# Converting the float64 weights in place: raw words in the slots of their halves, three word operations in a PSUM bank, and the first k and v issued by ACT

## The chip, the cores and the metric

The kernel runs on one core of one Trainium2 chip. The metric is the device time of the program in microseconds (us), the median over runs of the same program. A profile is one execution of it, recorded by the hardware profiler. Engines are called as in the profile: PE is TensorE (PEld its weight loads), DVE is VectorE, ACT is ScalarE, POOL is GpSimd, SP is SyncE, which here only issues DMAs.

## The reference: block-causal attention, then a feed-forward layer with a rational activation

```
scores = (q @ k^T) / 8                     # 8 batches x 8 heads, 576 tokens, head size 64
scores = where(block_i >= block_j, scores, -1e9)      # blocks of 64 tokens
attn   = exp(scores - max);  attn = attn / (sum(attn) + 1e-9)
x      = (attn @ v) -> 4608 tokens x 512
h      = x @ w_in                          # 512 x 2048, w_in and w_out are float64
g      = (a0 + a1 h + a2 h^2 + a3 h^3) / (1 + |b0||h| + |b1|h^2 + 1e-6)
out    = g @ w_out                         # 2048 x 512
```

q, k and v are float32. The weights arrive as float64, and the kernel reads them as pairs of 32-bit words: w0 is the low word and w1 the high one.

## The kernel before

**Attention.** The 64 heads are taken as 32 pairs of two. A pair has five row tiles (in the order 4, 3, 2, 0, 1) and two heads, which makes ten steps (`items`, L636), and `attn_steps` (L638) runs through them. For each step PE computes a score tile into a PSUM bank of the pool `ps_a` (five banks), DVE takes the row maximum out of it (L511, or L507 for the last half of tile 4), ACT takes the exponential with its sum (L522), POOL adds the guard to the sum (L530), DVE inverts it (L531), and POOL scales the row (L534). PE then transposes the probabilities (L560) into a bank that `bank` (L464) hands out, and for the first six pairs ACT copies the bank to SBUF (L571) and PE multiplies it in full float32 with v (L583, L587). For later pairs the probabilities are split into a high and a low half. `load` (L363) fetches q and k of a pair, `prep` (L401) transposes and splits them, and `vprep` (L441) fetches or splits v; all DMAs go out on SP's queue. For the first four pairs `bank` cycles through four sources: `ps_a`, the two banks of `ps_o` and the one bank of `ps_h`. Up to twelve pairs also issue three dummy matmuls before a transpose (L557).

**Feed-forward.** It has two phases over the hidden dimension: phase A takes the first 1280 of 2048 columns (NFA = 10 blocks of 128) in chunks of 256 tokens, and runs among the attention steps; phase B takes the remaining 768 (NFB = 6 blocks) in chunks of 512 tokens after the attention. One unit of phase A computes h (`first`, L192, matmuls on L204, into the one bank of `ps_h`, tag "a"), which ACT and DVE read (L211, L213, L219, L220), then the activation, then `second` (L255, matmuls on L272). x and g and the weights are each split into a high and a low fp32r half, and three of the four products are taken. Phase A starts at step 52, when the first batch (four pairs) has its x in DRAM (`xscr`).

**The weights.** A "place" is one quarter of two 128-blocks: 128 partitions by 512 float64 values, 512 KB. Phase A has 20 places and phase B 12. `split_weights` (L114) handles a place as follows. SP loads the raw words into a staging tile (tag "os", two buffers, shared with the output tiles; L121). ACT takes the absolute value of the high words as floats (L126) into the tile `at` (tag "u", two buffers). DVE then works on `at` in SBUF: a maximum with the smallest allowed exponent (L127), a shift with a mask (L129), the upper three bits of the low word shifted in (L131), and the sign put back (L133). ACT writes the rounded high half (L138) and POOL subtracts to get the low half (L139). For phase B the two halves go to DRAM (L143 to L146) and come back after the attention (L722). The main loop (L699) asks for a place at chosen steps: phase A's at steps 9, 18, 27, 36 and then 44 to 59, phase B's from step 80 on.

**What sets the order.** The engines' instruction orders are fixed when the program is built: the framework simulates the program and puts on each engine, at every moment, the first instruction in program order whose inputs and buffers are ready. So an instruction can stand well ahead of its place in the program if its buffers are free, and a conversion stands ahead of its step wherever the staging tiles let it. At run time every engine, and SP's queue too, works strictly in that order.

Of the kernel before, what the change touches and what calls it, by code (L numbers as in the profile page):

```python
# [2 lines left out]

# [6 lines left out]
F32 = mybir.dt.float32  # L10
F32R = mybir.dt.float32r
I32 = mybir.dt.int32
U32 = mybir.dt.uint32
AF = mybir.ActivationFunctionType
ALU = mybir.AluOpType
# [4 lines left out]
B, H, S, D = 8, 8, 576, 64  # L20
# [6 lines left out]
LEND = 4  # L27
RL = 3
C0 = 0
EV = 6  # L30
DP = 12
DN = (3, 0, 0, 0, 0)
# [16 lines left out]
NFA = 10  # L49
# [9 lines left out]
MASKS = ((None, None), (0, 0), (0, 1), (1, 0))  # L59
QC = 1.0 + 1e-6  # L60

WMIN = struct.unpack("<f", struct.pack("<I", (1023 - 127) << 20))[0]


@with_exitstack
def attn_ffn_kernel(
# [39 lines left out]
    b0, b1 = bab[:, 0:1], bab[:, 1:2]  # L106


    def weight_tiles(pool, f0, nf, dt):
        wi = [pool.tile([128, 4, nf * 128], dt, name=f"wi{x}{f0}", tag=f"wi{x}") for x in "hl"]  # L110
        wo = [pool.tile([128, nf, DM], dt, name=f"wo{x}{f0}", tag=f"wo{x}") for x in "hl"]
        return wi + wo

    def split_weights(pool, f0, nf, dt):  # L114
        wih, wil, woh, wol = weight_tiles(pool, f0, nf, dt)

        def place(dhi, dlo, src, nm):

            nd, n = src.shape[1:]
            st = ffn.tile([128, 512, 2], I32, name=f"st{nm}", tag="os")  # L120
            nc.sync.dma_start(out=st.rearrange("p (d f) t -> p d (f t)", d=nd), in_=src.bitcast(I32))  # L121
            w0, w1 = st[:, :, 0], st[:, :, 1]
            at = ffn.tile([128, 512], F32, name=f"wa{nm}", tag="u")
            ai = at.bitcast(I32)

            nc.scalar.activation(out=at, in_=w1.bitcast(F32), func=AF.Abs)  # L126
            nc.vector.tensor_scalar_max(at, at, WMIN)  # L127

            nc.vector.tensor_scalar(out=ai, in0=ai, scalar1=3, scalar2=0x3FFFFFF8,  # L129
                                    op0=ALU.logical_shift_left, op1=ALU.bitwise_and)  # L130
            nc.vector.scalar_tensor_tensor(out=ai, in0=w0, scalar=29, in1=ai,  # L131
                                           op0=ALU.logical_shift_right, op1=ALU.bitwise_or)
            nc.vector.scalar_tensor_tensor(out=ai, in0=w1, scalar=-0x40000000, in1=ai,  # L133
                                           op0=ALU.bitwise_and, op1=ALU.bitwise_or)

            v3 = lambda x: x.rearrange("p (d f) -> p d f", d=nd)
            if dt is F32R:
                nc.scalar.copy(out=dhi, in_=v3(at))  # L138
                nc.gpsimd.tensor_tensor(out=dlo, in0=v3(at), in1=dhi.bitcast(F32), op=ALU.subtract)  # L139
            else:  # L140
                bt = ffn.tile([128, 512], F32R, name=f"wb{nm}", tag="v")
                pt = ffn.tile([128, 512], F32R, name=f"wp{nm}", tag="s")
                nc.scalar.copy(out=bt, in_=at)  # L143
                nc.gpsimd.tensor_tensor(out=pt, in0=at, in1=bt.bitcast(F32), op=ALU.subtract)
                nc.sync.dma_start(out=dhi, in_=v3(bt).bitcast(F32))
                nc.sync.dma_start(out=dlo, in_=v3(pt).bitcast(F32))  # L146

        def steps():
            for f in range(0, nf, 2):
                cs = slice(f * 128, f * 128 + 256)  # L150
                for d in range(0, 4, 2):
                    src = w_in[d * 128:(d + 2) * 128, (f0 + f) * 128:(f0 + f + 2) * 128]
                    place(wih[:, d:d + 2, cs], wil[:, d:d + 2, cs],
                          src.rearrange("(d p) f -> p d f", p=128), f"i{f0}_{f}_{d}")
                    yield
                for d in range(f, f + 2):
                    place(woh[:, d:d + 1, :], wol[:, d:d + 1, :],
                          w_out[(f0 + d) * 128:(f0 + d + 1) * 128, :].rearrange("(d p) e -> p d e", p=128),
                          f"o{f0}_{d}")
                    yield  # L160

        return (wih, wil, woh, wol), steps()


    class Ffn:
# [24 lines left out]
                self.x[ph, c] += [x[:, d] for d in range(nd)]  # L190

        def first(self, ph, c, u):  # L192
            wih, wil, _, _ = self.w[ph]
            xs = self.x[ph, c]
            tag = f"{ph}_{c}_{u}"
            pool = self.pools[self.n % len(self.pools)]
# [1 line left out]
            h = hp.tile([128, NBU[ph], CTS[ph]], F32, name=f"h{tag}", tag="a", bufs=1 if hp is ps_h else 3)  # L198
            for j in range(NBU[ph]):
                f = NBU[ph] * u + j  # L200
                fs = slice(f * 128, (f + 1) * 128)
                for dc in range(4):
                    for i, (w, hl) in enumerate(((wih, 1), (wih, 0), (wil, 0))):
                        nc.tensor.matmul(h[:, j, :], lhsT=w[:, dc, fs], rhs=xs[dc][:, hl, :],  # L204
                                         start=(dc == 0 and i == 0), stop=(dc == 3 and i == 2))
            self.n += 1
            hf = h.rearrange("p j t -> p (j t)")
# [45 lines left out]
                nc.gpsimd.tensor_tensor(out=gl, in0=st, in1=gh.bitcast(F32), op=ALU.subtract)  # L253

        def second(self, ph, c, u):  # L255
            _, _, woh, wol = self.w[ph]
            gh, gl = self.g.pop((ph, c, u))
            nu = NU[ph]
            nm = CTS[ph] // 128
# [7 lines left out]
            for j in range(NBU[ph]):  # L267
                f = NBU[ph] * u + j
                for m in range(nm):
                    ms = slice(m * 128, (m + 1) * 128)  # L270
                    for i, (g, w) in enumerate(((gh, woh), (gh, wol), (gl, woh))):
                        nc.tensor.matmul(self.o[m], lhsT=g[:, j, ms], rhs=w[:, f, :],  # L272
                                         start=(u == 0 and j == 0 and i == 0),
                                         stop=(u == nu - 1 and j == NBU[ph] - 1 and i == 2))
            if u == nu - 1:
# [53 lines left out]
    with ExitStack() as actx:  # L329
# [33 lines left out]
        def load(p):  # L363
            b, hp = divmod(p, NPAIR)
            h0 = 2 * hp
            qr, kr = ((ffn.tile([128, 4, 2, D], F32, name=f"{n}r{p}", tag="x", bufs=XB) if p < RL else
                       att.tile([128, 4, 2, D], F32, name=f"{n}r{p}", tag="raw", bufs=2)) for n in "qk")
            tr = att.tile([128, 2, D], F32, name=f"tr{p}", tag="tr", bufs=1)
            if p >= EV:
                vr = att.tile([128, 2, 5, D], F32, name=f"vr{p}", tag="vr", bufs=1)  # L370
            for i, (raw, src) in enumerate(((qr, q), (kr, k))):
                for j in range(2):
                    nc.sync.dma_start(out=raw[:, :, j, :],
                                      in_=src[b, h0 + j, 0:512, :].rearrange("(c p) d -> p c d", p=128))
                nc.sync.dma_start(out=tr[64 * i:64 * i + 64], in_=src[b, h0:h0 + 2, 512:S, :].rearrange("j p d -> p j d"))
            if p < EV:
                st_[p] = dict(qr=qr, kr=kr, tr=tr)
                return
            for j in range(2):
                nc.sync.dma_start(out=vr[:, j, 0:4, :],  # L380
                                  in_=v[b, h0 + j, 0:512, :].rearrange("(c p) d -> p c d", p=128))
            nc.sync.dma_start(out=vr[0:64, :, 4, :], in_=v[b, h0:h0 + 2, 512:S, :].rearrange("j p d -> p j d"))
            st_[p] = dict(qr=qr, kr=kr, tr=tr, vr=vr)
# [57 lines left out]
        def vprep(p):  # L441
            if p < EV:
                b, hp = divmod(p, NPAIR)
                for j in range(2):
                    js, src = slice(64 * j, 64 * j + 64), v[b, 2 * hp + j]
                    nc.sync.dma_start(out=vz[:, 0:4, j, js], in_=src[0:512].rearrange("(c p) d -> p c d", p=128))
                    nc.sync.dma_start(out=vz[0:64, 4, j, js], in_=src[512:S])
                return
            if p == EV:
                late()  # L450
# [13 lines left out]
        def bank(p, name):  # L464

            if p < LEND:
                nbank[0] += 1
                pool, tag = ((ps_a, "a"), (ps_o, "o0"), (ps_o, "o1"), (ps_h, "a"))[nbank[0] % 4]
            else:
                pool, tag = ps_a, "a"  # L470
            return pool.tile([128, 512], F32, name=name, tag=tag)
# [196 lines left out]
                yield k  # L668
            assert not todo

        wts, wsteps = split_weights(wpool, 0, NFA, F32R)
        load(0)
        for _ in range(C0):
            next(wsteps)
# [1 line left out]
        prep(0, 1)  # L676
        vprep(0)
        ff = Ffn()
        ff.w[0] = wts
        fsteps = ff.steps()  # L680
        done = 0

# [5 lines left out]
                done += 1  # L688

        KB = NPAIR * 10  # L690
        wscr, wstepsB = split_weights(dpool, NFA, NFB, F32)
        NWA, NWB = 2 * NFA, 2 * NFB
        wdone = C0
        WSTEPS = [0] * C0 + [(W0 * (i + 1)) // 4 for i in range(4 - C0)] + [WA + WD * i // 4 for i in range(NWA - 4)]
# [16 lines left out]

    wB = ctx.enter_context(tc.tile_pool(name="wB", bufs=1))
    ffb = ctx.enter_context(tc.tile_pool(name="ffb", bufs=2))
    wtsB = weight_tiles(wB, NFA, NFB, F32R)
    ff.w[1] = wtsB
    ff.ready = NCH
    ps_b = ctx.enter_context(tc.tile_pool(name="ps_b", bufs=1, space=PSUM))
    ff.pools, ff.hpools = [ffn, ffb], [ps_h, ps_b]
    for f in range(0, NFB, 2):
        for i, (d, s) in enumerate(zip(wtsB, wscr)):  # L720
            at = (slice(None), slice(None), slice(f * 128, f * 128 + 256)) if i < 2 else (slice(None), slice(f, f + 2))
            nc.sync.dma_start(out=d[at].bitcast(F32), in_=s[at])  # L722
    for _ in fsteps:
        pass

# [29 lines left out]
```

## Time and profile before

| what | value |
|---|---|
| median of 3 runs (lowest, highest) | 1302.56 us (1300.33, 1307.7) |
| the profiled execution, its span | 1301.48 us, 1299.6 us |
| PE busy | 1252.8 us (96% of the span) |
| DVE, ACT, POOL busy | 71%, 71%, 69% |
| mean granted TensorE clock | 0.994 of full |
| conversion of a phase A place begins on ACT | at 14.4 us the first, at 131.6 us the last |
| conversion of phase B's places ends | at about 606 us |

The span runs from the first to the last instruction. "Busy" is the time in which an engine executes; matmul ends are modelled. An idle stretch of an engine is put down to the releaser that came last. In the view of windows each row gives, for a stretch of time, the busy time of every engine with its number of instructions, the granted clock, the busy share of the DMA engines and their rate.

### The profile page before, as it was taken

The numbers are of one execution on the slowest core, as the hardware profiler recorded it, in microseconds if no ns is written. First come the engines' busy times: TensorE is split into PE (matmuls) and PEld (weight loads), VectorE is DVE, ScalarE is ACT, GpSimd is POOL, SyncE is SP. The second block draws the span as 40 slices with busy tenths as digits, with TensorE's granted clock in tenths as the row PEclk, the third lists the DMA queues.
The fourth block names the chain that finished last, engine by engine and source line by source line (L and its number), as shares of the span: only waits on it lengthen the run. The fifth ranks groups of instructions, "written<-read, shape, count | busy, mean of one in ns | idle before, by whom it ended". The sixth has DMA issues, their size and how long they took to land.

```text
span 1299.6 us, 22697 instructions
## 1 busy us (share of the span) xinstructions
PE 1252.8 (96%) x7644; PEld 1058.3 (81%) x7644; DVE 923.2 (71%) x1735; ACT 927.8 (71%) x2047; POOL 895.6 (69%) x1041
## 2 busy tenths in 40 slices
PE   6879899999999999999999999999999999999997
PEld 4657788888878888888888888897998888888886
DVE  5896667776887768778667677754656776666765
ACT  5776778877788777878868777876776655555553
POOL 4665668777777778787767676766677666666564
PEclk8999899999999999999999999999999999999999
DMA  6675243544443453543434333247111333443423
GB/s 156 179 203 146 67 138 87 142 114 139 123 114 96 137 151 93 151 114 100 116 82 111 90 84 96 72 145 264 61 49 49 107 105 130 130 130 130 147 81 106
DMA packets 210355, 153.80 MB, mean 118 GB/s; under 512 B 137792, under 2 KB 176704, under 8 KB 210240
## 3 DMA queue, kind: packets, MB, share of 16 engines
q1 hardware_dynamic: 210176, 152.36, 40.3%
q8 instruction: 61, 1.00, 0.3%
q14 instruction: 54, 0.44, 0.1%
q0 software_dynamic: 64, 0.00, 0.0%
HBM read 98.57 MB, written 44.04 MB: 110 GB/s over the span
## 4 chain that ended last, share of the span: by engine, by line
PE 74%; DVE 8%; ACT 7%; POOL 5%; DMA 3%; issue 2%; SPq 2%; POOLq 0%; ACTq 0%; DVEq 0%
PE h L204 28%; PE o L272 27%; PE o L626 5%; PE t L560 4%; PE s L500 3%; PE s L497 2%; ACT p L522 2%; PE tp L410 1%; DVE nm L511 1%; POOL p L534 1%; PE s L484 1%; PE o L587 1%; DMA x<-xscr 1%; POOL u L238 1%; POOL gl L250 1%
## 5 line engine op out<-in xcount | busy, mean ns | idle before, releaser
L204 PE MATMUL h<-x,wih 128*128 128x256 f32 (+1 forms) x1872 | 415.6, 313 | 3.0 <-DMA x<-xscr 2.2
L204 PEld LDWEIGHTS h<-x,wih 128*128 128x128 f32 x1872 | 309.2, 190 | 30.6 <-issue 5.0
L204 PE MATMUL h<-x,wil 128*128 128x256 f32 (+1 forms) x936 | 290.7, 311 | 0.0
L272 PE MATMUL o<-woh,gh 128*128 128x512 f32 x576 | 229.2, 398 | 1.5 <-ACT os L282 1.3
L272 PE MATMUL o<-wol,gh 128*128 128x512 f32 x576 | 226.6, 393 | 0.0
L272 PE MATMUL o<-woh,gl 128*128 128x512 f32 x576 | 214.6, 400 | 2.0 <-POOL gl L250 1.8
L534 POOL TENSOR_SCALAR p<-p,rc 128x128 f32<-128x128 f32 (+4 forms) x288 | 178.7, 632 | 49.9 <-DVE rc L531 44.8
L522 ACT ACTIVATE p<-s,nm 128x288 f32<-128x288 f32 (+4 forms) x320 | 167.6, 532 | 59.1 <-DVE nm L511 54.0
L218 POOL TENSOR_TENSOR u<-v,u 128x512 f32<-128x512 f32 x144 | 187.0, 1299 | 32.2 <-ACT v L214 27.3
L204 PEld LDWEIGHTS h<-x,wil 128*128 128x128 f32 x936 | 178.2, 190 | 9.3
L219 DVE TENSOR_TENSOR s<-s,h 128x512 f32<-128x512 f32 x144 | 98.4, 683 | 118.2 <-ACT s L213 59.4
L238 POOL TENSOR_TENSOR u<-s,u 128x512 f32<-128x512 f32 x90 | 116.4, 1293 | 69.1 <-DVE u L236 54.5
L226 ACT ACTIVATE v<-u,qcb 128x512 f32<-128x512 f32 x144 | 105.0, 729 | 73.4 <-POOL u L218 73.3
L211 ACT ACTIVATE u<-h 128x512 f32<-128x512 f32 x144 | 86.0, 597 | 91.1 <-PE h L204 83.2
L511 DVE TENSOR_REDUCE nm<-s 128x1 f32<-128x128 f32 (+4 forms) x288 | 128.2, 477 | 21.7 <-PE s L500 16.8
L560 PE MATMUL t<-ident,p 128*128 128x128 f32 x800 | 125.1, 279 | 7.8 <-POOL p L534 3.8
L272 PEld LDWEIGHTS o<-woh,gh 128*128 128x128 f32 x576 | 108.3, 188 | 24.3 <-ACT os L282 2.4
L272 PEld LDWEIGHTS o<-woh,gl 128*128 128x128 f32 x576 | 104.4, 188 | 26.0 <-POOL gl L250 4.8
L272 PEld LDWEIGHTS o<-wol,gh 128*128 128x128 f32 x576 | 108.3, 188 | 20.3
L574 DVE TENSOR_TENSOR ptrl<-t,ptrh 128x512 fp32r<-128x512 f32 (+1 forms) x182 | 111.6, 626 | 17.4 <-ACT ptrh L573 16.3
L250 POOL TENSOR_TENSOR gl<-u,v 128x512 fp32r<-128x512 f32 x90 | 119.4, 1326 | 2.9
L560 PEld LDWEIGHTS t<-ident,p 128*128 128x128 f32 x800 | 92.7, 141 | 28.6 <-issue 6.0
(107 smaller groups left out, 2511.3 us busy)
## 6 DMA issues: line engine op xcount, KB each, us to landing
x<-xscr SPq DMA_DIRECT2D x56, 256.0 KB, 3.6
xscr<-xl SPq DMA_DIRECT2D x32, 288.0 KB, 2.3
pscr<-os SPq DMA_DIRECT2D x18, 512.0 KB, 2.8
pt<-pscr SPq DMA_DIRECT2D x36, 256.0 KB, 4.3
out_dram<-os SPq DMA_DIRECT2D x36, 256.0 KB, 3.5
qr<-in_q_dram SPq DMA_DIRECT2D x64, 128.0 KB, 2.6
kr<-in_k_dram SPq DMA_DIRECT2D x64, 128.0 KB, 2.5
sti<-in_moe_w_in_dram SPq DMA_DIRECT2D x16, 512.0 KB, 3.9
```

The costliest lines, as they stand in the source:

```text
L204: nc.tensor.matmul(h[:, j, :], lhsT=w[:, dc, fs], rhs=xs[dc][:, hl, :], start=(dc == 0 and i == 0), stop=(dc == 3 and i == 2))
L218: nc.gpsimd.tensor_tensor(out=ut, in0=vt, in1=ut, op=ALU.mult)
L219: nc.vector.tensor_tensor(out=st, in0=st, in1=hf, op=ALU.mult)
L226: nc.scalar.activation(out=vt, in_=ut, func=AF.Ln, bias=qcb)
L238: nc.gpsimd.tensor_tensor(out=ut, in0=st, in1=ut, op=ALU.subtract)
L250: nc.gpsimd.tensor_tensor(out=gl, in0=ut, in1=vt, op=ALU.mult)
L272: nc.tensor.matmul(self.o[m], lhsT=g[:, j, ms], rhs=w[:, f, :], start=(u == 0 and j == 0 and i == 0), stop=(u == nu - 1 and j == NBU[ph] - ...
L511: nc.vector.reduce_max(out=nm[:, j:j + 1], in_=s[d, j][:, :w], axis=AX.X, negate=True)
L522: nc.scalar.activation(out=dst, in_=s.pop((d, j2))[:, :w], func=AF.Exp, bias=nm[:, n:n + 1], scale=1.0, accum_out=sm[:, j2:j2 + 1])
L534: nc.gpsimd.tensor_scalar(out=x, in0=x, scalar1=rc[:, j2:j2 + 1], scalar2=1.0, op0=ALU.mult, op1=ALU.mult)
L560: nc.tensor.transpose(ps[:, 128 * x:128 * x + 128], src[:, 128 * kb:128 * kb + 128], ident)
L574: nc.vector.tensor_tensor(out=dl, in0=src, in1=dh.bitcast(F32), op=ALU.subtract)
```

## The change

Three things change.

1. **Raw words in the slots of their own halves.** The weights' tiles are cut into one tile of 4 KB per partition for each place (high half, then low half, 512 values each). For phase A the raw words are loaded straight into that slot, since 1024 words fill it exactly, and the halves overwrite them once the word operations have read them. There is no staging tile for phase A any more; instead the load of a place waits, by a dependency added by hand, for the last word operation of the place four before it (RW = 4). Phase B still uses the staging tiles, and its DRAM scratch has the new layout, so that each place comes back in one DMA of 512 KB.
2. **Three word operations instead of four.** ACT's absolute value gets a scale of 2^-112, which puts the exponent where it belongs, so the maximum and the mask go. For phase A the intermediate `ab` lies in a PSUM bank, the one of `ps_h`: ACT writes it, the shift works on it in place, the low word's bits are put in in place, and the sign operation reads it and writes `at` in SBUF. For phase B the intermediate stays in SBUF. `bank` no longer uses `ps_h`: for the first four pairs it cycles through three sources.
3. **The first k and v from ACT's queue.** For pair 0 the three DMAs of k and the four of v are issued by ACT and not by SP.

The matmuls read the same numbers of columns from the new tiles; their count and shapes do not change.

```
+RW = 4
-WMIN = struct.unpack("<f", struct.pack("<I", (1023 - 127) << 20))[0]
+WSCALE = 2.0 ** -112
...
+        def slot(self, key, dt, raw):
+            x, f, d = key
+            nm = f"{x}{self.f0}_{f}_{d}"
+            return self.pool.tile([128, 2, 512], dt, name=f"w{'r' if raw else 'p'}{nm}", tag=f"w{nm}", bufs=1)
...
+        def convert(self):
+            last = []
+            for key in self.places:
...
+                raw = self.slot(key, I32, True) if there else ffn.tile([128, 2, 512], I32, name=f"st{nm}", tag="os")
+                nd = 2 if x == "i" else 1
+                got = nc.sync.dma_start(out=raw.rearrange("p a (d f) -> p (a d f)", d=nd).rearrange("p (d f) -> p d f", d=nd),
+                                        in_=src.bitcast(I32).rearrange("(d p) f -> p d f", p=128))
+                if there and len(last) >= RW:
+                    tc.add_manual_dep(got.ins, last[-RW].ins.name,
+                                      mybir.DependencyInfo(mybir.DependencyClass.Sync, mybir.DependencyReason.DATA),
+                                      reason="order")
+                words = raw.rearrange("p a f -> p (a f)").rearrange("p (f t) -> p f t", t=2)
+                w0, w1 = words[:, :, 0], words[:, :, 1]
+                at = ffn.tile([128, 512], F32, name=f"wa{nm}", tag="u")
+                ab = ps_h.tile([128, 512], F32, name=f"wc{nm}", tag="a") if there else at
+                ai, bi = at.bitcast(I32), ab.bitcast(I32)
+                nc.scalar.activation(out=ab, in_=w1.bitcast(F32), func=AF.Abs, scale=WSCALE)
+                nc.vector.tensor_scalar(out=bi, in0=bi, scalar1=3, scalar2=None, op0=ALU.logical_shift_left)
+                nc.vector.scalar_tensor_tensor(out=bi, in0=w0, scalar=29, in1=bi,
+                                               op0=ALU.logical_shift_right, op1=ALU.bitwise_or)
+                last.append(nc.vector.scalar_tensor_tensor(out=ai, in0=w1, scalar=-0x80000000, in1=bi,
+                                                           op0=ALU.bitwise_and, op1=ALU.bitwise_or))
+                if there:
+                    w = self.tile(key)
+                    nc.scalar.copy(out=w[:, 0], in_=at)
+                    nc.gpsimd.tensor_tensor(out=w[:, 1], in0=at, in1=w[:, 0].bitcast(F32), op=ALU.subtract)
...
             for i, (raw, src) in enumerate(((qr, q), (kr, k))):
+                eng = nc.scalar if p == 0 and i == 1 else nc.sync
...
         def vprep(p):
...
+                eng = nc.scalar if p == 0 else nc.sync
...
         def bank(p, name):
...
-                pool, tag = ((ps_a, "a"), (ps_o, "o0"), (ps_o, "o1"), (ps_h, "a"))[nbank[0] % 4]
+                pool, tag = ((ps_a, "a"), (ps_o, "o0"), (ps_o, "o1"))[nbank[0] % 3]
...
-    for f in range(0, NFB, 2):
-        for i, (d, s) in enumerate(zip(wtsB, wscr)):
-            at = (slice(None), slice(None), slice(f * 128, f * 128 + 256)) if i < 2 else (slice(None), slice(f, f + 2))
-            nc.sync.dma_start(out=d[at].bitcast(F32), in_=s[at])
+    for key in wscr.places:
+        nc.sync.dma_start(out=ff.w[1].tile(key).bitcast(F32), in_=wscr.tile(key))
```

More of the change, by code (lines that the diff above doesn't have):

```diff
@@ L1 @@
-import struct
 from contextlib import ExitStack
@@ L106, in attn_ffn_kernel @@
     b0, b1 = bab[:, 0:1], bab[:, 1:2]
[L109 to L162, printed above, removed]
@@ new lines, in attn_ffn_kernel, with __init__, tile, win @@
+    class Weights:
+        def __init__(self, pool, f0, nf, dt):
+            self.pool, self.f0, self.dt = pool, f0, dt
+            self.places = [x for f in range(0, nf, 2) for x in (("i", f, 0), ("i", f, 2), ("o", f, 0), ("o", f + 1, 0))]
+            self.t = {}
+        def slot(self, key, dt, raw):
+            x, f, d = key
+            nm = f"{x}{self.f0}_{f}_{d}"
+            return self.pool.tile([128, 2, 512], dt, name=f"w{'r' if raw else 'p'}{nm}", tag=f"w{nm}", bufs=1)
+        def tile(self, key):
+            if key not in self.t:
+                self.t[key] = self.slot(key, self.dt, False)
+            return self.t[key]
+        def win(self, f, dc, y):
+            c = 256 * (dc % 2) + 128 * (f % 2)
+            return self.tile(("i", f // 2 * 2, dc // 2 * 2))[:, y, c:c + 128]
+        def wout(self, f, y):
+            return self.tile(("o", f, 0))[:, y]
+        def convert(self):
+            last = []
+            for key in self.places:
+                x, f, d = key
+                f += self.f0
+                src = w_in[d * 128:(d + 2) * 128, f * 128:(f + 2) * 128] if x == "i" else w_out[f * 128:f * 128 + 128]
+                nm = f"{x}{f}_{d}"
+                there = self.dt is F32R
+                raw = self.slot(key, I32, True) if there else ffn.tile([128, 2, 512], I32, name=f"st{nm}", tag="os")
[21 more added lines that the diff above has]
+                    nc.gpsimd.tensor_tensor(out=w[:, 1], in0=at, in1=w[:, 0].bitcast(F32), op=ALU.subtract)
+                else:
+                    bt = ffn.tile([128, 512], F32R, name=f"wb{nm}", tag="v")
+                    pt = ffn.tile([128, 512], F32R, name=f"wp{nm}", tag="s")
+                    nc.scalar.copy(out=bt, in_=at)
+                    nc.gpsimd.tensor_tensor(out=pt, in0=at, in1=bt.bitcast(F32), op=ALU.subtract)
+                    for y, z in enumerate((bt, pt)):
+                        nc.sync.dma_start(out=self.tile(key)[:, y], in_=z.bitcast(F32))
+                yield
@@ L192, in first @@
         def first(self, ph, c, u):
-            wih, wil, _, _ = self.w[ph]
             xs = self.x[ph, c]
@@ L200, in first @@
                 f = NBU[ph] * u + j
-                fs = slice(f * 128, (f + 1) * 128)
                 for dc in range(4):
-                    for i, (w, hl) in enumerate(((wih, 1), (wih, 0), (wil, 0))):
-                        nc.tensor.matmul(h[:, j, :], lhsT=w[:, dc, fs], rhs=xs[dc][:, hl, :],
+                    for i, (y, hl) in enumerate(((0, 1), (0, 0), (1, 0))):
+                        nc.tensor.matmul(h[:, j, :], lhsT=self.w[ph].win(f, dc, y), rhs=xs[dc][:, hl, :],
                                          start=(dc == 0 and i == 0), stop=(dc == 3 and i == 2))
@@ L255, in second @@
         def second(self, ph, c, u):
-            _, _, woh, wol = self.w[ph]
             gh, gl = self.g.pop((ph, c, u))
@@ L270, in second @@
                     ms = slice(m * 128, (m + 1) * 128)
-                    for i, (g, w) in enumerate(((gh, woh), (gh, wol), (gl, woh))):
-                        nc.tensor.matmul(self.o[m], lhsT=g[:, j, ms], rhs=w[:, f, :],
+                    for i, (g, y) in enumerate(((gh, 0), (gh, 1), (gl, 0))):
+                        nc.tensor.matmul(self.o[m], lhsT=g[:, j, ms], rhs=self.w[ph].wout(f, y),
                                          start=(u == 0 and j == 0 and i == 0),
@@ L371, in load @@
             for i, (raw, src) in enumerate(((qr, q), (kr, k))):
+                eng = nc.scalar if p == 0 and i == 1 else nc.sync
                 for j in range(2):
-                    nc.sync.dma_start(out=raw[:, :, j, :],
+                    eng.dma_start(out=raw[:, :, j, :],
                                       in_=src[b, h0 + j, 0:512, :].rearrange("(c p) d -> p c d", p=128))
-                nc.sync.dma_start(out=tr[64 * i:64 * i + 64], in_=src[b, h0:h0 + 2, 512:S, :].rearrange("j p d -> p j d"))
+                eng.dma_start(out=tr[64 * i:64 * i + 64], in_=src[b, h0:h0 + 2, 512:S, :].rearrange("j p d -> p j d"))
             if p < EV:
@@ L443, in vprep @@
                 b, hp = divmod(p, NPAIR)
+                eng = nc.scalar if p == 0 else nc.sync
                 for j in range(2):
                     js, src = slice(64 * j, 64 * j + 64), v[b, 2 * hp + j]
-                    nc.sync.dma_start(out=vz[:, 0:4, j, js], in_=src[0:512].rearrange("(c p) d -> p c d", p=128))
-                    nc.sync.dma_start(out=vz[0:64, 4, j, js], in_=src[512:S])
+                    eng.dma_start(out=vz[:, 0:4, j, js], in_=src[0:512].rearrange("(c p) d -> p c d", p=128))
+                    eng.dma_start(out=vz[0:64, 4, j, js], in_=src[512:S])
                 return
@@ L669, in attn_steps @@
             assert not todo
-        wts, wsteps = split_weights(wpool, 0, NFA, F32R)
+        wA = Weights(wpool, 0, NFA, F32R)
+        wsteps = wA.convert()
         load(0)
@@ L678, in attn_ffn_kernel @@
         ff = Ffn()
-        ff.w[0] = wts
+        ff.w[0] = wA
         fsteps = ff.steps()
@@ L690, in attn_ffn_kernel @@
         KB = NPAIR * 10
-        wscr, wstepsB = split_weights(dpool, NFA, NFB, F32)
+        wscr = Weights(dpool, NFA, NFB, F32)
+        wstepsB = wscr.convert()
         NWA, NWB = 2 * NFA, 2 * NFB
@@ L713, in attn_ffn_kernel @@
     ffb = ctx.enter_context(tc.tile_pool(name="ffb", bufs=2))
-    wtsB = weight_tiles(wB, NFA, NFB, F32R)
-    ff.w[1] = wtsB
+    ff.w[1] = Weights(wB, NFA, NFB, F32R)
     ff.ready = NCH
```

## The prediction

> **What bounds the kernel now.** I read the page first: the busy shares and the forty slices.
>
> ```profile
> PE 1252.8 (96%) x7644; PEld 1058.3 (81%) x7644; DVE 923.2 (71%) x1735; ACT 927.8 (71%) x2047; POOL 895.6 (69%) x1041
> ...
> PE   6879899999999999999999999999999999999997
> ...
>
> ```
>
> PE is busy nearly everywhere; only the first four or five slices (32.5 us each) fall short, and there DVE shows its own peak. So the kernel is bound by PE, and what can be won lies at the start. The view of windows, cut where the first h unit begins (106 us) and where PE's idling ends (140 us), puts numbers to it. Its columns are the stretch and its length, then busy us of PE, PEld, DVE, ACT and POOL, the granted clock, the DMA share and GB/s.
>
> ```profile
> 0.00:20.00 20.00, 11.10 (x53) 7.88 (x54) 9.64 (x25) 8.91 (x23) 5.81 (x22) 1.00 0.78 184
> 20.00:106.00 86.00, 72.14 (x431) 52.43 (x429) 72.10 (x154) 60.54 (x174) 58.64 (x85) 0.96 0.64 183
> 106.00:140.00 34.00, 28.21 (x177) 21.88 (x175) 27.01 (x51) 23.82 (x61) 18.93 (x28) 0.96 0.35 100
> 140.00:870.00 730.00, 721.13 (x4908) 620.07 (x4909) 535.58 (x1112) 579.55 (x1382) 541.80 (x679) 1.00 0.40 110
> 870.00:910.00 40.00, 37.46 (x239) 32.71 (x238) 18.98 (x26) 26.24 (x42) 26.77 (x21) 1.00 0.79 282
> 910.00:1299.60 389.60, 382.74 (x1847) 323.31 (x1845) 259.84 (x368) 228.73 (x370) 243.65 (x209) 1.00 0.31 102
> ```
>
> PE idles 8.9 us before 20 us, 13.9 us between 20 and 106, and 5.8 us between 106 and 140. That is 28.6 of the 47 us that it idles in all. Between 20 and 106 DVE is as busy as PE (72.1 of 86 us). What comes off the start comes off the end, since the 721.1 of 730 us behind it do not change. The ceiling for the stretch from 20 to 140 us is its 19.7 us of idle PE; the clock of 0.96 could give back at most 4% of 120 us, 4.8 us.
>
> What DVE does in that time, from the view of groups of the first 160 us (count, then busy us and mean ns):
>
> ```profile
> L133 DVE SCALAR_TENSOR_TENSOR wao<-sto,wao 128x512 int32<-128x512 int32 x10 | 10.6, 1056 | 0.0
> L131 DVE SCALAR_TENSOR_TENSOR wai<-sti,wai 128x512 int32<-128x512 int32 x10 | 9.5, 950 | 0.3
> L131 DVE SCALAR_TENSOR_TENSOR wao<-sto,wao 128x512 int32<-128x512 int32 x10 | 9.4, 937 | 0.1
> L133 DVE SCALAR_TENSOR_TENSOR wai<-sti,wai 128x512 int32<-128x512 int32 x10 | 7.8, 777 | 0.2
> L129 DVE TENSOR_SCALAR wai<-wai 128x512 int32<-128x512 int32 x10 | 7.3, 726 | 0.1
> ...
> L127 DVE TENSOR_SCALAR wai<-wai 128x512 f32<-128x512 f32 x10 | 6.7, 674 | 3.9 <-ACT wai L126 3.9
> L129 DVE TENSOR_SCALAR wao<-wao 128x512 int32<-128x512 int32 x10 | 5.6, 556 | 0.1
> ...
> L127 DVE TENSOR_SCALAR wao<-wao 128x512 f32<-128x512 f32 x10 | 5.4, 535 | 4.4 <-ACT wao L126 4.4
> ```
>
> The twenty conversions of phase A cost DVE 62.3 us, 3.1 us a place, and they lie on the path. The chain of waits between 20 and 140 us says how much:
>
> ```profile
> by line: DVE nm L511 7.9%; POOL p L534 6.8%; DMA sti<-in_moe_w_in_dram 6.4%; ACT p L522 5.6%; issue 5.6%; DVE wai L131 4.8%; PE o L587 4.7%; DVE wao L133 4.2%; DMA sto<-in_moe_w_out_dram 3.9%; DVE wai L129 3.6%; ACT pt L571 3.4%; DVE wai L1
> ...
> 24.18 4.70 DMA sto<-in_moe_w_out_dram
> ...
> 54.45 3.84 DMA sti<-in_moe_w_in_dram
> 78.64 3.85 DMA sti<-in_moe_w_in_dram
> ```
>
> The three conversion groups that it names hold 12.6% of 120 us, 15.1 us, out of 27.4 us that these groups are busy: 55% of the conversion's DVE time is on the path. The loads of raw words hold another 10.3%, 12.4 us, three of them as whole landings of about 4 us.
>
> **The change, part by part.**
>
> *Word operations.* Each place loses one of four (L127) and the rest move. The nearest rows to the new ones are in phase B of the feed-forward layer, where DVE combines an SBUF and a PSUM operand and writes SBUF (L242) or PSUM (L243), and ACT writes PSUM (L241). They give lowest, median and highest ns:
>
> ```profile
> L129 DVE TENSOR_SCALAR wao<-wao x10: 416/488/1031, 28.0 to 132.7; 128x512 int32<-128x512 int32 x10
> ...
> L242 DVE SCALAR_TENSOR_TENSOR u<-u,r x54: 675/681/690, 1003.7 to 1286.7; 128x512 f32<-128x512 f32 x54
> ...
> L243 DVE SCALAR_TENSOR_TENSOR r<-u,r x54: 685/695/697, 1004.9 to 1287.4; 128x512 f32<-128x512 f32 x54
> ...
> L241 ACT ACTIVATE r<-v x54: 591/602/604, 1002.9 to 1286.0; 128x512 f32<-128x512 f32 x54
> ```
>
> With one operand in PSUM the spread is 15 ns over 54 instructions, though POOL works 243.7 of 389.6 us there. With both in SBUF the means above run from 777 to 1056 ns. So I cost the sign at 0.68 us and the low bits at 0.695. The shift has no row of its own: between 0.416 (the old shift undisturbed in SBUF) and 0.695 (L243). I take 0.695, since the place of the operands decides more here than their number. A place then costs 2.07 us, twenty cost 41.4 us, and DVE saves 20.9 us (26.5 with the lower value). Half of it on the path, a little under the 55%, is 10 us. Bounds: 5 us if the attention's own steps take over half of those places, 15 with all of the path's share and the cheap shift.
>
> The Trainium skill, VectorE: DVE Perf Modes, in "Why PSUM operands drop a tier", speaks against this move: an fp32 operand in PSUM takes the doubled rate from a single-source operation, so leaving SBUF makes the shift itself slower. Its cycle table gives, as an estimate, (120 + 512) / 0.96 = 658 ns, by which DVE would save 21.6 us. The means of 556 and 726 ns of the old shift beside POOL say that the doubled rate is not kept there anyway; no row shows the shift in PSUM.
>
> ACT's absolute value goes into PSUM, by L241 at 0.60 us, and POOL's subtraction stays. Both engines are at 68 to 70% between 20 and 106 us: taken as nothing; if they are the bound, it is the second rival.
>
> *Loads.* SP is held up by the two staging tiles. In the view of SP's waits before 160 us:
>
> ```profile
> SPq L121 <- DVE wao L133: 14.1, 5, 6.4
> ```
>
> Behind such a wait stand q and k of the next pair and the stores of x. With slots of their own and a lead of four places, the landings leave the path unless DVE falls behind. What is late next is DVE's queue itself, so only part of the 12.4 us turns into time: I take a third, 4 us, between 0 and 12.
>
> *The bank taken from the transposes.* `bank` is called ten times a pair (three in `prep`, seven in `transp`). For four pairs `ps_a` gets a third of these instead of a quarter, 3.3 for 2.5, beside ten score tiles and two outputs: 6% more tiles through five banks. PE's waits for a bank before 160 us:
>
> ```profile
> PE s L497 <- ACT p L522: 4.8, 9, 1.2
> ...
> PE t L560 <- ACT p L522: 2.4, 2, 1.5
> ```
>
> 6% of 7.2 us is 0.4 us; at worst they double. I take 1.5 us lost.
>
> *The start.* The timeline of the first microseconds, by start and length:
>
> ```profile
> 0.73 1.28 ACT L79 ACT_TABLE_LOAD   x1 [0.73 <-PEq L739]
> ...
> 2.55 1.14 SPq L373 DMA_DIRECT2D kr<-in_k_dram  x2
> ...
> 3.75 1.17 POOL L349 MEMSET vz<- 128x1280 f32 x1
> ...
> 5.68 0.58 ACT L390 ACTIVATE q<-tp 128x512 fp32r<-128x512 f32 x1
> ...
> 6.69 1.08 PE L410 MATMUL tp<-ident,kr 128*128 128x128 f32 x4 [1.84 <-DMA kr<-in_k_dram]
> ...
> 10.47 0.60 SPq L121 DMA_DIRECT2D sti<-in_moe_w_in_dram  x1
> ```
>
> On ACT the k loads can go out when the table is in, at 2.0 us instead of 2.55: 0.5 us won at most. The four v loads write a tile that POOL clears until 4.92 us. ACT waits there with q's split queued behind it, and four issues of about 0.57 us each end at 7.2: 1.5 us late for q, though k's split, which follows its transposes at 7.8 us, is the later one. I take 0.5 us lost, between 0.5 won and 1.5 lost. SP loses seven issues, some 4 us, so the first weights go out near 6 us instead of 10.5, up to four of them at once. They travel with pair 1's k: 1 MB more at the 184 GB/s of the first 20 us would be 5.7 us if that load had to wait for all of it; only part will stand ahead of it, and I take 1 us, between 0 and 5.7.
>
> The Trainium skill, DMA: Bandwidth & Descriptors, in "Issuing engines are not separate DMA queues", says that issuing from several engines saves only issue time, since all share the same sixteen engines. By it this edit is worth the 0.5 us and no bandwidth, and nothing in the sum changes sign; the DMA share of 0.78 fits.
>
> *Phase B.* Twelve places lose L127 too, but PE is busy 721.1 of 730 us there: nothing. The halves come back in longer rows; PE idles 2.5 us between 870 and 910, so at most about 1 us, taken as nothing.
>
> Sum: -10 - 4 + 1.5 + 0.5 + 1 = -11 us. On the profiled execution's 1301.48 us this gives 1290.5; the median shown is 1.1 us above it, so the forecast is **1291.5 us**.
>
> **The rivals.** *PE takes over at once.* DVE's saving and the loads together (20.9 + 12.4) exceed PE's 19.7 idle us. If PE then runs as it does from 140 us on, at 721.1/730, it keeps 1.4 of them: 18 us won, with the costs above left out 1284. For it: the size. Against it: ACT, POOL and DVE hand each row's softmax on one after the other (L511, L522 and L534 hold 20% of the chain).
>
> *The next chain.* Those softmax steps set the pace as soon as the conversions thin out, and the conversion's ACT and POOL steps are not shortened. Then only a quarter of the 20.9 us counts, 5 us, the landings count nothing, and the costs of 3 us remain: 2 us won, 1300. The same time comes out if the shift and sign in PSUM still collide with POOL, at the old mean of 0.95 us; L242 speaks against that.
>
> *The single bank.* Conversions and the h units of phase A share one bank.
>
> ```profile
> 113.84 0.68 ACT L126 ACTIVATE wai<-sti 128x512 f32<-128x512 f32 x1
> ...
> 131.56 0.67 ACT L126 ACTIVATE wao<-sto 128x512 f32<-128x512 f32 x1
> ...
> 109.29 1.94 PE h L204 x14
> ...
> 115.30 0.74 DVE L220 SCALAR_TENSOR_TENSOR s<-s,coef,h 128x512 f32<-128x512 f32 x1
> ```
>
> An h unit holds it from 109.3 to 116.0 us, 6.7 us. An absolute value that waits for it stops ACT, and behind it the exponentials and the copies of the transposes. Before, four conversions came after the first unit. If three of them wait out a whole unit, ACT loses 20 us, and with the gain of 10 the kernel ends 10 us later, 1312. It decides once more than half of these late conversions meet a unit. Against it: earlier loads should bring most conversions ahead of 106 us.
>
> **How the numbers follow.** Forecast 46%, PE takes over 14%, next chain 28%, single bank 12%. This kernel's measurement can tell about 0.5% from no change, 6.5 us. The forecast's own range is 1284 to 1297: the bounds of the word operations shift it by 5 us either way and the loads give a little more. Nearly all of it is faster by over 6.5 us; with PE's case that makes 58%. The next chain and the forecast's upper edge give 30% within 0.5%, the bank 12% slower. The range runs from 1282, below PE's case, to 1305, past the next chain, and leaves out the bank's case and a few per cent beneath.
>
> **What would show it.** Right: no conversion operation on DVE above 0.70 us, their sum near 41 us, no landing of weights in the chain, the last conversion begun near 115 us instead of 131.6, the first h unit near 97 us instead of 109, and some 9 us of idle PE between 20 and 140. Wrong: PE waits for ACT's exponentials growing by several us, ACT's absolute values waiting for h, pair 1's k landing after PE wants it, or word operations in PSUM still running at a microsecond.

## The result, and the profile after

The changed kernel takes 1286.73 us (median of 4 runs, 1286.31 to 1287.41) against 1303.32 for the kernel before in the same comparison: a ratio of 0.9876 with a 95% interval of 0.9847 to 0.9904, 16.6 us faster. The profiled execution took 1287.04 us, its span is 1285.3.

The row of DVE in the slices of the kernel before, which the prediction reads but does not show, was this:

```profile
DVE  5896667776887768778667677754656776666765
```

And the page of the changed kernel:

```profile
PE 1255.0 (98%) x7644; PEld 1059.5 (82%) x7644; DVE 904.0 (70%) x1703; ACT 925.3 (72%) x2047; POOL 880.5 (69%) x1041
...
PE   7989999999999999999999999999999999999997
...
DVE  5767678777777777777767676754666767666675
```

PE's first five slices rose from 6, 8, 7, 9, 8 to 7, 9, 8, 9, 9, and DVE's peak of 8 and 9 in the second and third slice is down to 7 and 6. The view of windows in the prediction's stretches:

```profile
0.00:20.00 20.00, 13.42 (x54) 9.53 (x55) 8.95 (x25) 8.60 (x24) 5.79 (x22) 1.00 0.88 221
20.00:106.00 86.00, 79.24 (x483) 58.57 (x481) 62.72 (x151) 67.02 (x191) 52.30 (x93) 1.00 0.70 199
106.00:140.00 34.00, 33.07 (x210) 25.88 (x211) 24.00 (x55) 26.21 (x72) 23.06 (x33) 1.00 0.30 82
140.00:870.00 730.00, 722.39 (x4908) 621.72 (x4907) 535.72 (x1091) 577.34 (x1367) 537.58 (x672) 1.00 0.41 114
870.00:910.00 40.00, 38.43 (x241) 33.59 (x240) 19.81 (x27) 28.07 (x45) 26.14 (x20) 1.00 0.44 166
910.00:1285.30 375.30, 368.46 (x1756) 310.26 (x1754) 252.79 (x359) 218.06 (x353) 235.65 (x204) 1.00 0.32 105
```

PE's idle time fell by 2.3 us before 20 us, by 7.1 between 20 and 106, by 4.9 between 106 and 140 and by 2.2 between 140 and 910: 16.5 us together, 14.3 of them before 140. PE's busy time grew by 2.2 us, so the span fell by 14.3 us, from 1299.6 to 1285.3. DVE is busy 62.7 us instead of 72.1 in the second stretch, while PE does 483 matmuls there and not 431. The word operations, from the groups of the first 160 us:

```profile
L154 DVE TENSOR_SCALAR wci<-wci 128x512 int32<-128x512 int32 x10 | 7.0, 698 | 5.0 <-ACT wci L153 5.0
L155 DVE SCALAR_TENSOR_TENSOR wco<-wro,wco 128x512 int32<-128x512 int32 x10 | 6.9, 694 | 0.2
L154 DVE TENSOR_SCALAR wco<-wco 128x512 int32<-128x512 int32 x10 | 6.9, 694 | 1.8 <-ACT wco L153 1.8
L155 DVE SCALAR_TENSOR_TENSOR wci<-wri,wci 128x512 int32<-128x512 int32 x10 | 6.9, 692 | 0.2
L157 DVE SCALAR_TENSOR_TENSOR wai<-wri,wci 128x512 int32<-128x512 int32 x10 | 6.8, 683 | 0.2
L157 DVE SCALAR_TENSOR_TENSOR wao<-wro,wco 128x512 int32<-128x512 int32 x10 | 6.8, 680 | 0.1
```

On average all of them take 0.68 to 0.70 us, 41.3 us in all. In the chain of waits from 20 to 140 us no load of weights is among the long pieces any more. PE has taken the lead, and the DMAs that remain bring q and k or carry x out to DRAM and back; here are the chain's shares by line, its longest pv group (pv is the product of the probabilities with v) and some landings around it:

```profile
by line: PE o L594 14.2%; DMA xscr<-xl 6.7%; PE h L210 6.2%; ACT p L529 6.2%; PE t L567 5.9%; DMA qr<-in_q_dram 3.7%; ACT pt L578 3.6%; PE s L507 3.6%; DMA kr<-in_k_dram 3.3%; issue 3.2%; DVE wai L157 2.8%; DVE wci L155 2.8%; DVE wci L154 2
...
66.67 3.92 DMA kr<-in_k_dram
...
83.25 4.45 DMA qr<-in_q_dram
88.03 5.62 PE o L594 x20
95.19 2.75 DMA xscr<-xl
98.00 2.62 DMA x<-xscr
```

The last conversion begins at 120.1 us on ACT, where it was 131.6, and the first h unit at 100.7 us, where it was 109.3. (The 106 us of the prediction's cut is where that unit's x began to load.)

### The profile page after: what moved, and what is told of

Read it like the earlier page. It is cut to its first block, busy times and chain, and to the rows that moved or that the text cites. A ratio compares the mean times of both kernels' runs of the same rounds, so it can differ in the third digit from the quotient of the medians.

```text
span 1285.3 us, 22748 instructions
## 1 busy us (share of the span) xinstructions
PE 1255.0 (98%) x7644; PEld 1059.5 (82%) x7644; DVE 904.0 (70%) x1703; ACT 925.3 (72%) x2047; POOL 880.5 (69%) x1041
## 4 chain that ended last, share of the span: by engine, by line
PE 82%; ACT 7%; DVE 4%; DMA 3%; POOL 3%; issue 1%; SPq 0%; ACTq 0%; POOLq 0%; DVEq 0%
PE h L210 30%; PE o L277 28%; PE o L633 6%; PE t L567 5%; PE s L507 4%; PE s L504 3%; ACT p L529 2%; PE tp L416 2%; PE s L491 1%; PE o L594 1%; DMA x<-xscr 1%; PE o L617 1%; DMA xscr<-xl 1%; POOL u L244 1%; ACT s L219 1%
## 5 line engine op out<-in xcount | busy, mean ns | idle before, releaser
L210 PE MATMUL h<-x,wpi 128*128 128x256 f32 (+1 forms) x2808 | 462.8, 312 | 3.1 <-DMA x<-xscr 1.7
L210 PEld LDWEIGHTS h<-x,wpi 128*128 128x128 f32 x2808 | 396.4, 190 | 40.6 <-issue 4.0
L277 PE MATMUL o<-wpo,gh 128*128 128x512 f32 x1152 | 351.0, 397 | 1.3 <-ACT os L287 1.3
L277 PEld LDWEIGHTS o<-wpo,gh 128*128 128x128 f32 x1152 | 211.1, 188 | 43.7 <-ACT os L287 1.8
L277 PE MATMUL o<-wpo,gl 128*128 128x512 f32 x576 | 213.8, 401 | 1.2 <-POOL gl L256 1.1
L244 POOL TENSOR_TENSOR u<-s,u 128x512 f32<-128x512 f32 x90 | 116.7, 1297 | 72.1 <-DVE u L242 58.1
L277 PEld LDWEIGHTS o<-wpo,gl 128*128 128x128 f32 x576 | 104.3, 189 | 23.5 <-POOL gl L256 3.3
L259 POOL TENSOR_TENSOR gl<-s,gh 128x512 fp32r<-128x512 f32 x54 | 69.9, 1294 | 62.9 <-ACT gh L258 62.9
L580 ACT CAST ptrh<-t 128x512 fp32r<-128x512 f32 (+1 forms) x182 | 95.7, 545 | 18.8 <-PE t L567 18.2
L226 DVE SCALAR_TENSOR_TENSOR s<-s,coef,h 128x512 f32<-128x512 f32 x144 | 107.2, 744 | 2.9
L507 PE MATMUL s<-k,q 64*128 64x512 f32 (+3 forms) x768 | 103.5, 351 | 0.0
```

Of the source, the lines that this page charges most:

```text
L210: nc.tensor.matmul(h[:, j, :], lhsT=self.w[ph].win(f, dc, y), rhs=xs[dc][:, hl, :], start=(dc == 0 and i == 0), stop=(dc == 3 and i == 2))
L226: nc.vector.scalar_tensor_tensor(out=st, in0=st, scalar=a1, in1=hf, op0=ALU.add if ph == 0 else ALU.subtract, op1=ALU.mult)
L244: nc.gpsimd.tensor_tensor(out=ut, in0=st, in1=ut, op=ALU.subtract)
L277: nc.tensor.matmul(self.o[m], lhsT=g[:, j, ms], rhs=self.w[ph].wout(f, y), start=(u == 0 and j == 0 and i == 0), stop=(u == nu - 1 and j = ...
L507: mm = nc.tensor.matmul(s[d, h][:, :w], lhsT=q[hs, x, 128 * i:128 * i + 128], rhs=k[hs, y, 0:w], start=(n == 0), stop=(n == 3), skip_group ...
```

## The experiments

Two theories of where the time came from, W (the word operations in PSUM) and L (the loads), and a third, S (the start), were put to single undoings first. Ratios are to the kernel before, with their intervals; 0.001 is 1.3 us.

**Start undone** (own order).

```
-                eng = nc.scalar if p == 0 and i == 1 else nc.sync
-                eng = nc.scalar if p == 0 else nc.sync
+                eng = nc.sync
```

> The changed kernel with the first k and v issued by SP again. Theory W (the gain of 16.6 us is mostly DVE time, from the word operations in PSUM): about 2 us given back, 1288 to 1289.5. Theory L (mostly the loads, early and without a staging tile): 2 to 3 us, since the first weights go out later as well. Theory S (the earlier start, 1.1 us from the transposes of k and a PE that is warm sooner, spreads through the whole early stage): 5 us or more, 1292 and up.

Measured: 1293.17 us, 0.9921 (0.9897 to 0.9945). About 6 us given back, more than W and L had asked for.

**Word operations in SBUF** (own order).

```
-                ab = ps_h.tile([128, 512], F32, name=f"wc{nm}", tag="a") if there else at
+                ab = at
```

> The changed kernel with the intermediate of phase A's word operations in SBUF: three operations as now, but in the tile that the result goes to; the loads, the start and the three-source bank stay. By the old rows the shift then takes some 0.64 us and the two others some 0.93 each, 2.5 us a place instead of 2.06, 9 us more on DVE in all. Theory W: about half of that is given back, 4 to 5 us, 1291. Theory L: under 1.5 us, 1287 to 1288. If the means of the two-input operations stay at 0.69 us with POOL beside them, the price of two SBUF operands that I took from the old rows was something else.

Measured: 1314.54 us, 1.0087 (1.0062 to 1.0111): 27 us given back and slower than before, far outside every theory.

**Loads through staging tiles** (own order).

```
-                raw = self.slot(key, I32, True) if there else ffn.tile(...)
+                raw = ffn.tile(...)
-                if there and len(last) >= RW:
+                if False:
```

> The changed kernel with phase A's raw words loaded through the two staging tiles again and no dependency by hand; word operations in PSUM, start and bank stay. Theory W: 3 to 4 us given back, 1290 to 1291. Theory L: 8 us or more, 1295 and up, and landings of weights are back in the chain.

Measured: 1303.59 us, 0.9997 (0.9982 to 1.0012): the whole gain is gone, though the word operations still take 0.68 to 0.70 us. Its chain of waits shows something else than loads:

```profile
69.52 7.30 PE o L594 x20
90.12 7.30 PE o L594 x20
114.25 7.30 PE o L594 x20
```

A group of twenty pv matmuls takes 7.30 us where the changed kernel's took 5.62. The granted clock of this run is 0.93 between 20 and 106 us, and 0.83 in the ten microseconds from 70, from 90 and from 110 us, where most of each of these groups runs. At 1.7 us a group that is some 5 of the 16 us.

**The start alone**, on the kernel before (own order): the first edit's two lines added there.

> The kernel before with nothing changed but the queue of the first k and v. Theory W: 1 to 2 us faster than before, about 1301.5; theory S: 5 us or more, 1298 and less.

Measured: 1307.25 us, 1.0024 (1.0009 to 1.0039), slower than before.

Undoing the three parts one at a time gives back 6, 27 and 16 us of a gain of 16.6. No sum of costs does that, so the theories fell. What the runs share is that each edit also changes what the program's simulation sees, and with it the order of the instructions on every engine: in the traces PE's row of matmuls, by line and tile, first departs from the changed kernel's at the 77th with staged loads and at the 150th with SBUF words. That is theory O: what the undoings gave back is the order's. Theory C says that it is the cost of the parts themselves. The next runs hold the order fixed. Each engine's instructions are tied one behind the other, without a semaphore, in the order of another kernel:

```
+        for eng, row in order_of_the_other_kernel.items():
+            for a, b in zip(row, row[1:]):
+                tc.add_manual_dep(b, a.name, mybir.DependencyInfo(mybir.DependencyClass.NoSync,
+                                  mybir.DependencyReason.DATA), reason="order")
```

In the traces of the runs so tied, all 7644 matmuls of PE stand in the order of the kernel that they were tied to.

**Word operations in SBUF, order of the changed kernel.**

> The word operations in SBUF as in the second experiment, but with every engine's and queue's instructions in the order of the changed kernel (dependencies without a semaphore tie each instruction to the one ahead of it). Theory O (what the single parts gave back came mostly from the other order that the program's simulation chose, with PE's clock falling in the pauses): near 1291, the 4 to 5 us that DVE's 9 us of longer operations are worth. Theory C (the costs of the parts themselves): near the 1314.5 of the second experiment, at least 1305.

Measured: 1298.03 us, 0.9952 (0.9937 to 0.9967): 0.0076 above the changed kernel, 10 us, and not 27. The groups of its first 160 us:

```profile
L154 DVE TENSOR_SCALAR wao<-wao 128x512 int32<-128x512 int32 x10 | 11.4, 1144 | 2.2 <-ACT wao L153 2.1
L155 DVE SCALAR_TENSOR_TENSOR wai<-wri,wai 128x512 int32<-128x512 int32 x10 | 10.9, 1093 | 0.2
L154 DVE TENSOR_SCALAR wai<-wai 128x512 int32<-128x512 int32 x10 | 8.7, 873 | 6.7 <-ACT wai L153 6.7
L157 DVE SCALAR_TENSOR_TENSOR wai<-wri,wai 128x512 int32<-128x512 int32 x10 | 8.1, 812 | 0.2
L155 DVE SCALAR_TENSOR_TENSOR wao<-wro,wao 128x512 int32<-128x512 int32 x10 | 7.3, 729 | 0.2
L157 DVE SCALAR_TENSOR_TENSOR wao<-wro,wao 128x512 int32<-128x512 int32 x10 | 6.8, 681 | 0.1
```

The same three operations take 53.2 us instead of 41.3. The shift, which undisturbed would be the cheapest, takes 0.87 and 1.14 us on average. In the order of the second experiment they took less, 49.3 us, with the shift at 0.44 and 0.52 us, and that kernel was 16 us slower than this one. POOL becomes slower too; here are two of its groups, first in the changed kernel and then in this run:

```profile
L541 POOL TENSOR_SCALAR p<-p,rc 128x384 f32<-128x384 f32 x16 | 9.2, 585 | 2.1 <-DVE rc L538 1.5 <-DVE k L399 0.5
L537 POOL TENSOR_SCALAR rc<-sm 128x2 f32<-128x2 f32 x30 | 6.7, 224 | 16.6 <-ACT p L529 14.1 <-ACT xh L601 1.1
...
L541 POOL TENSOR_SCALAR p<-p,rc 128x384 f32<-128x384 f32 x14 | 9.9, 716 | 2.1 <-DVE rc L538 2.0
L537 POOL TENSOR_SCALAR rc<-sm 128x2 f32<-128x2 f32 x29 | 9.1, 315 | 17.7 <-ACT p L529 16.3
```

By the counts and means of all its softmax groups POOL works some 9 us longer for the same rows (an estimate). So 11.9 us of DVE time and some 9 us of POOL's, side by side, cost 10 us of the kernel's; the two intervals together leave 6 to 14 us. How much of it is DVE's and how much POOL's was not taken apart.

**Staged loads, a second look.**

> A look at the staged loads again, in the order that the simulation chose for them, beside the two that follow: 1300 to 1307, with PE's clock below 0.96 between 20 and 140 us under theory O as under theory C.

Measured: 1302.64 us in one run, as in the third experiment, with a clock of 0.91 between 20 and 106 us.

**Staged loads, order of the changed kernel.**

> Raw words through the two staging tiles, but PE, DVE, ACT and POOL in the order of the changed kernel (SP's order is left to the simulation). Theory O: under 1291. Theory C: 1300 and up, since the loads come no earlier than in the third experiment.

Measured: 1290.15 us, 0.9883 (0.9867 to 0.9898), 1 us above the changed kernel's ratio and within its interval; the two intervals together leave up to 5 us. The clock of its profiled execution (1290.92 us) is 0.91 between 20 and 106 us, no higher than with staged loads in their own order, so the mean clock does not set the two apart. With the changed kernel's order the staging tiles cost little, although SP's loads still wait for the word operations to free them (10.8 us in the largest group of these waits).

**The changed kernel in the order chosen for staged loads.**

> The changed kernel with its slots and its lead of four places, but PE, DVE, ACT and POOL in the order that the simulation chose for staged loads (SP's order is left to the simulation). Theory O: near 1303, the staged kernel's time. Theory C: near 1287, as changed. Between the two, with this and the run ahead of it adding up to about 17 us, the parts share it.

Measured: 1303.91 us, 0.9995 (0.9984 to 1.0006). Every instruction, slot and load of the change is there, and the gain is gone. This and the run ahead of it settle it: nearly all of the 16 us of the third experiment were the order's. Where it loses them, from the view of windows:

```profile
20.00:106.00 86.00, 76.99 (x451) 55.95 (x449) 60.08 (x144) 63.69 (x182) 50.08 (x89) 0.94 0.68 195
106.00:140.00 34.00, 30.74 (x184) 22.58 (x183) 23.24 (x51) 26.71 (x68) 20.14 (x30) 0.95 0.25 64
140.00:870.00 730.00, 717.22 (x4885) 616.24 (x4885) 537.10 (x1092) 571.85 (x1367) 539.83 (x673) 1.00 0.40 108
870.00:910.00 40.00, 33.98 (x215) 30.34 (x214) 16.43 (x23) 22.38 (x35) 22.13 (x17) 0.96 0.76 272
```

Beside the changed kernel PE idles 2.3, 2.3, 5.2 and 4.5 us more in these, the last around the step from phase A to phase B, and does 32 and 26 matmuls fewer in the first two. So more than half of the added idle time comes after 140 us.

**Start undone, order of the changed kernel.**

> The first k and v issued by SP again, PE, DVE, ACT and POOL in the order of the changed kernel. The first experiment gave back 6.5 us in an order of its own. Theory O: 1 to 2.5 us, 1288 to 1289. Theory C: 6.5 us again, 1293.

Measured: 1289.07 us, 0.9900 (0.9885 to 0.9915): 3 us above the changed kernel's ratio, not separable from it. A little under half of the first experiment's 6 us (2.7 us) goes with the order, but the intervals of the two runs overlap.

**All three undone, order of the changed kernel.**

> All three undone at once in the order of the changed kernel: staging tiles, intermediate in SBUF, first k and v from SP. What is left of the change is the operation fewer, the three-source bank and that order. If the parts add up at a fixed order: 1286.7 + 11.3 (words) + 3.4 (loads) + 2 (start), about 1303. If the time freed on DVE and the landings hide each other: about 1299.

Measured: 1297.17 us, 0.9958 (0.9945 to 0.9971): 0.0082 above the changed kernel, 11 us, no more than the word operations alone. The single prices at this order (10, 1 and 3 us) add up to 14, which the intervals do not separate from 11. It may be that the loads and the start are hidden while DVE is slow; that is not shown.

**The start alone on the kernel before, with that kernel's order.**

> The kernel before with the first k and v from ACT's queue, PE, DVE, ACT and POOL in the order of the kernel before. The fourth experiment, in an order of its own, came out 3.5 us slower than before. Theory O: that was the order, so with the old one no slower than before and up to 2 us faster, 1302 to 1304. Theory C: 3.5 us slower again.

Measured: 1300.51 us, 0.9986 (0.9974 to 0.9999): about 2 us faster, where the same edit with an order of its own was 3 us slower.

**A lead of eight places** (own order).

```
-RW = 4
+RW = 8
```

> The changed kernel with a lead of eight places instead of four, in its own order, which differs from the changed kernel's in one to six per cent of the instructions' places. The landings of weights are off the chain already, so the cost of the part itself should not move: 1286 to 1288 by theory C. Theory O: anything from 1284 to 1294, since even such a small reordering of the first 100 us moved the first experiment by several us.

Measured: 1289.22 us, 0.9901 (0.9888 to 0.9914), 3 us above the changed kernel's ratio, again not separable. No version that ran beats the changed kernel.

## Why the prediction was right, and which of its terms were not

**The bound and the ceiling.** Right. 14.3 of the 16.5 us of idle PE that went lay before 140 us, and the stretch behind it gave 2.2. Of the 19.7 us of idle PE between 20 and 140 us 7.7 are left (9 were forecast). Two signs came later than forecast: the last conversion began at 120.1 us, not near 115, and the first h unit at 100.7, not near 97.

**Word operations.** The durations held: 41.3 us for 41.4, and the shift, which had no row, took 0.69 to 0.70 us for 0.695. The Trainium skill's estimate of 0.658 us (VectorE: DVE Perf Modes, the cycle table in "The TRN2 errata") is 6% below. The Trainium skill's rule that PSUM drops the doubled rate (same page, "Why PSUM operands drop a tier") agrees with the trace, 0.69 to 0.70 us against 0.416 undisturbed in SBUF. Whether it points the wrong way depends on what POOL does meanwhile: the same shift in SBUF took 0.87 to 1.14 us in the changed kernel's order and 0.44 to 0.52 in the second experiment's. The Trainium skill, SBUF — State Buffer, in "Who interferes with whom", says why the place decides: an operation with two SBUF inputs, beside one of POOL that reads SBUF, or a single-source one at the doubled rate, contends with POOL for a shared port, and one with a single SBUF input at the plain rate does not; the trace agrees, for the two-input operations 0.68 to 0.69 us with PSUM, 0.68 to 1.09 with both in SBUF. Mis-sized may be the share on the path. I took half of the DVE time saved and put POOL at nothing; the fifth experiment gives 10 us for the place alone, without the operation fewer, but with POOL's rows slower too (0.585 to 0.716 us for 128x384; 0.761 in the kernel before). What POOL got back is a term that the sum left out, and no run prices it by itself.

**Loads.** Forecast 4 us between 0 and 12, measured about 1 us at a fixed order, near the lower bound, though the intervals do not exclude 4. The landings left the chain as forecast. What was late next was not DVE's queue, as the prediction has it: in the chain stand PE's pv groups (14.2%) and the landings of x, q and k (6.7, 3.7 and 3.3%).

**The bank.** Its 1.5 us were not tried alone. PE's waits for ACT's exponentials before 140 us are 2.2 us in all in the changed kernel, where two rows alone held 7.2 before, so nothing shows a loss.

**The start.** The step that failed in sign: "On ACT the k loads can go out when the table is in". The timeline of the changed kernel:

```profile
0.73 1.28 ACT L79 ACT_TABLE_LOAD   x1 [0.73 <-PEq L745]
...
0.76 1.06 ACTq L379 DMA_DIRECT2D kr<-in_k_dram  x2
...
5.29 1.06 PE L416 MATMUL tp<-ident,kr 128*128 128x128 f32 x4
...
6.57 0.20 ACT L100 ACTIVATE bab<-coef 128x2 f32<-128x2 f32 x1 [4.56 <-DMA coef<-in_moe_b_dram]
6.64 0.38 ACTq L453 DMA_DIRECT2D vz<-in_v_dram  x1
6.68 0.58 ACT L396 ACTIVATE q<-tp 128x512 fp32r<-128x512 f32 x1
```

They go out beside the table load, 1.8 us before the old 2.55, and k's transposes start at 5.3 us instead of 6.7. q's split is 1 us late all the same, but behind the coefficients' landing and not behind v. In place of 0.5 us lost stand 2 to 3 us won; only the 2 us on the kernel before are clear of zero by their interval, and narrowly. Pair 1's k was not crowded out either: its transposes run at 13.0 us, before they ran at 14.5.

**What the sum left out.** The sum took the order as given. It came out 5 us short, 11 for 16.6. 11 us is also what the three parts together are worth at the changed kernel's order, but that is no confirmation: the sum's 10 us for the words hold the operation fewer, and the measured 11 do not. The other 5.5 us (0.9958 against 1) are the operation fewer, the smaller bank rotation, phase B's layout and the difference between the two kernels' orders. These were not taken apart; the smaller rotation was not tried by itself. In the order chosen for staged loads the whole change is worth nothing (0.9995), so the 11 us hold for one order only, and another order alone cost up to 17 us (the second experiment against the fifth). That the total came near the sum is therefore partly luck. The measured time lies nearer to the rival in which PE takes over, 1284, than to the forecast; by the idle time that PE has left between 20 and 140 us, 7.7, it is the forecast (9) that fits, and not that rival (1.4).

**The rivals.** The next chain did not take over. The single bank did not either: four conversions came after the first unit, as before, and PE's h waited 0.2 us for a word operation.

## What to carry to other kernels

Where DVE and POOL work side by side, count how many of an operation's inputs lie in SBUF before counting operations. Here the intermediate of a chain in PSUM made the single-source step slower than it is undisturbed in SBUF (0.69 for 0.42 us), and still the three operations took 11.9 us less for twenty places at a fixed order, and POOL's rows beside them were shorter too. When a program's simulation orders the instructions, an edit is tried together with a new order, and here the order alone was worth 16 us, as much as the whole change. So tie the instructions to one order before reading a price off a single undoing, and remember that the price holds for that order.

## What was unexpected of the hardware

ACT's queue issued the k loads at 0.76 us, while ACT loaded its table from 0.73 to 2.01 us, and a v load at 6.64 us beside q's split from 6.68 on: in these two places the issue did not hold up the engine's own work. The granted clock fell to 0.93 between 20 and 106 us with staged loads, with pv groups of 7.30 instead of 5.62 us. At 70.3 and at 90.8 us of that run it went to 0.50 for 3.4 us, each time behind 3.4 us in which PE was busy for 1.7 to 1.8; in the changed kernel PE was busy for 2.0 of the 3.4 us before 70.3 us, and the clock stayed at 1.00. How much PE idles in the whole stretch does not say whether it falls: there PE idles 8.5 us at a clock of 1.00 with the start undone, and 9.0 us at 0.89 with the words in SBUF, both in the changed kernel's order. Nor does the mean clock give the time: executions of the changed kernel with 0.990 and with 0.998 differ by less than 0.1%, and staged loads in its order took 1290.92 us in an execution with 0.91 in that stretch.
